# Sliding-window attention on one core: score matmuls in eight tiles of 32 rows by 64 keys, and another order of the first quarter's Q and K

## The chip, the cores and the metric

The kernel runs on one core of one Trainium2 chip. The metric is the device time of that core in microseconds, from the launch to the last output byte. Engines are named as the profile names them: PE is the matmul engine and PEld its weight loads, DVE the vector engine, ACT the scalar engine, POOL the GpSimd engine, SP the engine that issues most transfers.

## The reference

Two independent problems A and B have the same shape: `x` is 2048 tokens by 1024 channels, `wqkv` 1024 by 3072, `wo` 1024 by 1024, all in bf16. Each is causal attention with 32 heads of 32 channels in a window of 256 keys; the two outputs stand side by side.

```python
H = 32; Dh = D // H; W = 256
qkv = ((x @ wqkv).reshape(B, S, 3, H, Dh)).transpose(2, 0, 3, 1, 4)
q, k, v = qkv[0], qkv[1], qkv[2]
scores = einsum("bhqd,bhkd->bhqk", q, k) * (Dh ** -0.5)
mask = (idx[:, None] - idx[None, :] >= 0) & (idx[:, None] - idx[None, :] < W)
scores = where(mask, scores, -1e9)
o = einsum("bhqk,bhkd->bhqd", softmax(scores), v)
return o.transpose(0, 2, 1, 3).reshape(B, S, D) @ wo
```

## The kernel before

The work is cut into 16 groups `g` (2 problems times 8), each of four heads: four heads of 32 channels fill 128 partitions. Tokens are cut into 16 blocks of 128. Keys stand on the partitions of a score tile and queries in its columns. A block `j` of keys meets the query blocks `q = j`, `j + 1` and `j + 2` alone; such a pair (g, j, q) is an entry. A group has 45 entries. Four entries at a time make a session, 180 in all.

`session(now)` computes one. It takes the score tile `st` (128 partitions, 4 heads, 4 entries, 128 queries in f32, four banks of PSUM, pool `ps_st` with one buffer). Entries of one key block that follow each other form a segment, with one matmul a head: 32 rows of `kT` and `qT` against 128 keys, at the row tile of that head (L451):

```python
for r in range(4):
    nc.tensor.matmul(
        st[:, r, a:b, :],
        lhsT=kT[32 * r:32 * r + 32, j * P:(j + 1) * P],
        rhs=qT[32 * r:32 * r + 32, q * P:(q + b - a) * P],
        start=True, stop=True, tile_position=(32 * r, 0))
```

A segment has one to three entries, so 128, 256 or 384 columns. In most sessions the segments are three and one, two and two, or one and three entries; twelve sessions at the seams of groups have three segments. ACT then takes the exponential of the whole tile into `pt` in bf16 (L459), and POOL clears what lies outside the mask in the entries with `q = j` (L467) and `q = j + 2` (L471). DVE adds the two edge blocks of a query block for the sums (L481).

`pv` multiplies the probabilities of a pair of query blocks by V and by ones (L513, column tiles of 32: each of the four heads writes its own 32 partitions). DVE normalises (L524, L529, L531). All projections (Q, K, V, output) accumulate in `pp`, a pool `ps_proj` of two banks. Their matmuls go through `by_columns`: whole 128x128 matmuls (L172), or, where a `pv` follows the session, four column tiles of 32 (L176). `evacuate` copies a finished `pp` to SBUF on ACT (L190) or DVE (L192), whichever a small clock in the program holds to be free earlier; `add_or` keeps a running OR of Q and K for a range test (L184).

The order of the instructions on each engine is written out by the program. For each session the loop emits the scores, then what `pv` and edge sums are due, then as many projection matmuls as `level` gives it from due times of chains (a chain is one accumulation over 8 channel tiles). Weights and x come by transfers that SP issues, planned by sessions too.

The head of the kernel has an order of its own. The first 512 tokens of A's x come as four row blocks `xrow[a]` and are transposed on PE (`flip`, L583), and ACT (L587) and DVE (L588) copy the halves of a transposed block to `xT`, one after the other. The other quarters come by transposing transfers (L133). `keep_warm` fills PE's waits with matmuls on zeros (L569), written to a part of the first `st` tile. The transfers stand in this order: Q's weights of group 0 on ACT's queue; on SP's queue x block 0, K's weights, x blocks 1 to 3, V's weights, the next quarter of x. Q and K of the first quarter (`first(a)`) are computed 128 tokens at a time behind each transposed block, Q then K, each accumulating in its own `pp` bank:

```python
flip(0); keep_warm(3); first(0)
flip(1); keep_warm(2); flip(2); first(1)
flip(3); first(2); first(3)
emit(0, chains[0].size)
```

The last line emits the first V chain. The sessions follow.

## Time and profile before

| what | value |
|---|---|
| median of 4 runs | 610.06 us (609.48 to 610.48) |
| the profiled execution | 610.16 us, span 608.4 us |
| PE busy, instructions | 598.9 us (98%), 12868 matmuls |
| PEld / DVE / ACT / POOL busy | 57% / 77% / 72% / 54% |
| score matmuls (L451) | 1488 |
| exponential (L459) | 180, 1878 ns each |
| first scores start | 14.27 us |

The span is what the profiler records from the first to the last instruction of the program; the profiled execution's time holds about 1.7 us more. A busy PE includes the tails of matmuls that overlap, so its share says who is busy and not how well; for the length of a stage, the starts of the matmuls are read. A group of instructions in the profile is given by its line, engine, operation, output and inputs.

### The profile page before, as it was taken

The numbers are of one execution on the slowest core, as the hardware profiler recorded it, in microseconds if no ns is written. First come the engines' busy times: TensorE is split into PE (matmuls) and PEld (weight loads), VectorE is DVE, ScalarE is ACT, GpSimd is POOL, SyncE is SP. The second block draws the span as 40 slices with busy tenths as digits, with TensorE's granted clock in tenths as the row PEclk, the third lists the DMA queues.
The fourth block names the chain that finished last, engine by engine and source line by source line (L and its number), as shares of the span: only waits on it lengthen the run. The fifth ranks groups of instructions, "written<-read, shape, count | busy, mean of one in ns | idle before, by whom it ended". The sixth has DMA issues, their size and how long they took to land.

```text
span 608.4 us, 28879 instructions
## 1 busy us (share of the span) xinstructions
PE 598.9 (98%) x12868; PEld 344.5 (57%) x12868; DVE 469.0 (77%) x1200; ACT 440.6 (72%) x375; POOL 326.2 (54%) x630
## 2 busy tenths in 40 slices
PE   8999999999999999999999999999999999999996
PEld 5555466656655756564556756655455665545443
DVE  2577889998898898897888887898888887887200
ACT  3777888788888887877778877777776777785332
POOL 0565666665666666556555565555555655554000
PEclk9999999999999999999999999999999999999998
DMA  9833110111015601553111100112021030113221
GB/s 236 181 88 91 37 39 3 38 37 39 3 38 90 118 9 28 86 96 80 37 37 38 38 4 10 31 37 81 2 64 37 6 104 20 56 62 115 72 78 64
DMA packets 86802, 35.47 MB, mean 58 GB/s; under 512 B 65552, under 2 KB 86160, under 8 KB 86672
## 3 DMA queue, kind: packets, MB, share of 16 engines
q1 hardware_dynamic: 85632, 33.31, 22.6%
q8 instruction: 102, 1.67, 1.1%
q10 hardware_dynamic: 1040, 0.26, 0.2%
q14 instruction: 28, 0.23, 0.1%
HBM read 17.83 MB, written 8.39 MB: 43 GB/s over the span
## 4 chain that ended last, share of the span: by engine, by line
PE 96%; ACT 2%; DMA 1%; SPq 0%; issue 0%; ACTq 0%
PE pp L176 43%; PE pp L172 29%; PE acc L513 13%; PE st L451 10%; ACT pt L459 1%; DMA oT<-in_A_x_dram 1%; PE acc L583 0%; ACT vt L190 0%; ACT kT L190 0%; ACT qT L190 0%; PE st L583 0%; PE st L569 0%; SPq L145 0%; SPq L548 0%; ACT osb L190 0%
## 5 line engine op out<-in xcount | busy, mean ns | idle before, releaser
L459 ACT ACTIVATE pt<-st 128x2048 bf16<-128x2048 f32 x180 | 338.0, 1878 | 91.9 <-PE st L451 72.7
L471 POOL TENSOR_SCALAR_AFFINE_SELECT pt<-pt 128x512 bf16<-128x512 bf16 x224 | 154.4, 689 | 145.5 <-ACT pt L459 144.0
L467 POOL TENSOR_SCALAR_AFFINE_SELECT pt<-pt 128x512 bf16<-128x512 bf16 x256 | 179.0, 701 | 86.5 <-ACT pt L459 85.6
L524 DVE RECIPROCAL rinv<-acc 128x128 f32<-128x128 f32 x128 | 121.9, 953 | 57.0 <-PE acc L513 56.5
L176 PE MATMUL pp<-xT,wqk 128*32 128x512 bf16 x2712 | 163.1, 379 | 0.0
L481 DVE TENSOR_TENSOR both<-pt 128x512 bf16<-128x512 bf16 x224 | 137.1, 651 | 0.0
L176 PEld LDWEIGHTS <-wqk 128*32 128x32 bf16 x2712 | 69.3, 97 | 54.2 <-issue 0.4
L172 PE MATMUL pp<-xT,wqk 128*128 128x512 bf16 (+1 forms) x394 | 83.4, 354 | 0.9 <-ACT vt L190 0.5
L176 PE MATMUL pp<-wv,xT 128*32 128x256 bf16 x2436 | 75.9, 273 | 0.0
L451 PE MATMUL st<-qT,kT 32*128 32x384 bf16 (+2 forms) x1488 | 71.5, 269 | 0.0
L176 PEld LDWEIGHTS <-xT 128*32 128x32 bf16 x2436 | 63.8, 97 | 6.1
L529 DVE STREAM_SHUFFLE wide<-rinv 128x128 f32<-128x128 f32 x256 | 64.6, 298 | 0.0
L513 PE MATMUL acc<-pt,vt 128*32 128x128 bf16 (+1 forms) x2160 | 63.3, 239 | 0.0
L172 PE MATMUL pp<-wo_sb,oT 128*128 128x512 bf16 (+1 forms) x282 | 61.2, 373 | 0.0
L451 PEld LDWEIGHTS <-kT 32*128 32x128 bf16 x1488 | 22.2, 92 | 64.5 <-issue 63.2
L190 ACT CAST osb<-pp 128x512 bf16<-128x512 f32 (+1 forms) x52 | 30.0, 576 | 39.1 <-PE pp L172 25.5
L531 DVE TENSOR_TENSOR oT<-acc,wide 128x256 bf16<-128x256 f32 x128 | 54.3, 424 | 4.4
L176 PE MATMUL pp<-wo_sb,oT 128*32 128x512 bf16 x952 | 55.6, 379 | 0.0
L172 PEld LDWEIGHTS <-wqk 128*128 128x128 bf16 x394 | 34.2, 98 | 37.5 <-issue 6.8
L172 PE MATMUL pp<-wv,xT 128*128 128x256 bf16 x415 | 50.9, 273 | 1.3 <-ACT kT L190 0.6
L513 PEld LDWEIGHTS <-vt 128*32 128x32 bf16 x2160 | 35.9, 96 | 26.4 <-issue 24.1
L172 PEld LDWEIGHTS <-xT 128*128 128x128 bf16 x415 | 39.0, 98 | 12.3 <-issue 6.4
(46 smaller groups left out, 385.0 us busy)
## 6 DMA issues: line engine op xcount, KB each, us to landing
out_dram<-osb SPq DMA_DIRECT2D x63, 128.0 KB, 1.8
wqk<-in_B_wqkv_dram SPq DMA_DIRECT2D x32, 128.0 KB, 2.6
wqk<-in_A_wqkv_dram SPq DMA_DIRECT2D x24, 128.0 KB, 2.8
wo_sb<-in_A_wo_dram SPq DMA_DIRECT2D x16, 128.0 KB, 2.2
wv<-in_B_wqkv_dram SPq DMA_DIRECT2D x16, 128.0 KB, 2.5
wo_sb<-in_B_wo_dram SPq DMA_DIRECT2D x16, 128.0 KB, 2.2
oT<-in_A_x_dram SPq DMA_DIRECT2D x4, 256.0 KB, 5.5
wv<-in_A_wqkv_dram SPq DMA_DIRECT2D x2, 512.0 KB, 5.9
```

The source lines that it names most:

```text
L172: nc.tensor.matmul(out[:, lo:hi], lhsT=lhsT, rhs=rhs, start=start, stop=stop, skip_group_check=True)
L176: nc.tensor.matmul(out[c:c + 32, lo:hi], lhsT=lhsT[:, c:c + 32], rhs=rhs, start=start, stop=stop, tile_position=(0, c), skip_group_check=True)
L190: nc.scalar.copy(out=out, in_=in_)
L451: nc.tensor.matmul(st[:, r, a:b, :], lhsT=kT[32 * r:32 * r + 32, j * P:(j + 1) * P], rhs=qT[32 * r:32 * r + 32, q * P:(q + b - a) * P], st ...
L459: nc.scalar.activation(out=pt[:, :, :n, :].rearrange("p r a q -> p r (a q)"), in_=st[:, :, :n, :].rearrange("p r a q -> p r (a q)"), func= ...
L467: nc.gpsimd.affine_select(out=blk, in_=blk, pattern=[[0, 4], [1, P]], compare_op=ALU.is_ge, fill=0.0, base=0, channel_multiplier=-1)
L471: nc.gpsimd.affine_select(out=blk, in_=blk, pattern=[[0, 4], [-1, P]], compare_op=ALU.is_gt, fill=0.0, base=0, channel_multiplier=1)
L481: nc.vector.tensor_tensor(out=both[:, :, h, :], in0=pts[s0][:, :, a0, :], in1=pts[s1][:, :, a1, :], op=ALU.add)
L513: nc.tensor.matmul(acc[32 * r:32 * r + 32, o:o + w_], lhsT=lhsT, rhs=src[:, r, :, :], start=(x == 0), stop=(x == len(moves) - 1), tile_pos ...
L524: nc.vector.reciprocal(out=rinv[:], in_=acc[:, 2 * P:3 * P])
L529: nc.vector.stream_shuffle(out=wide[:, h * P:(h + 1) * P], in_=rinv[:], mask=[16 * h] * 32)
L531: nc.vector.tensor_tensor(out=oTs[(pi, k)][:, t, (p % 2) * 256:(p % 2 + 1) * 256], in0=acc[:, 0:256], in1=wide[:], op=ALU.mult)
```

## The change

The score matmul of a segment and head becomes two, one for each half of its 128 keys. A half has a tile of 32 rows by 64 columns of the array and writes 64 partitions, so a segment has eight tiles. Each half goes over just the queries that it can meet: the upper 64 keys leave out the first 64 queries of an entry with `q = j`, the lower 64 keys the last 64 queries of an entry with `q = j + 2`. The score tile is one tile for the whole kernel, `scores`, cleared once by two memsets on DVE; the parts left out hold earlier scores, which the exponential covers and POOL clears with the mask.

In the head, `keep_warm` writes to a `pp` tile. K's weights are transferred behind x block 1 in place of ahead of it. Q and K of the first quarter are computed 256 tokens at a time: the first two transposes, Q's first half, the other two transposes, K's first half, then Q's and K's second halves. Lines behind line 19 of the new kernel are moved by a few; its scores are L458, its exponential L466, its P·V L520.

```diff
+HALF = 64
...
-        st = ps_st.tile([P, 4, SLOTS, P], F32, name="st")
+        st = scores
+        flat = st[:].rearrange("p r a q -> p r (a q)")
...
-            for r in range(4):
-                nc.tensor.matmul(
-                    st[:, r, a:b, :],
-                    lhsT=kT[32 * r:32 * r + 32, j * P:(j + 1) * P],
-                    rhs=qT[32 * r:32 * r + 32, q * P:(q + b - a) * P],
-                    start=True, stop=True, tile_position=(32 * r, 0))
+            for c in range(2):
+                lo = HALF if c == 1 and q == j else 0
+                hi = (b - a) * P - (HALF if c == 0 and q + b - a == j + 3 else 0)
+                keys = slice(j * P + c * HALF, j * P + (c + 1) * HALF)
+                for r in range(4):
+                    rows = slice(32 * r, 32 * r + 32)
+                    nc.tensor.matmul(
+                        flat[c * HALF:(c + 1) * HALF, r, a * P + lo:a * P + hi],
+                        lhsT=kT[rows, keys], rhs=qT[rows, q * P + lo:q * P + hi],
+                        start=True, stop=True, tile_position=(32 * r, c * HALF),
+                        skip_group_check=True)
...
-        if a == 0:
+        if a == 1:
             load_wqk(0, 1, nc.sync)
...
-    spare = ps_st.tile([P, 4, SLOTS, P], F32, name="st")[:].rearrange("p r a q -> p r (a q)")
-    warm = spare[:, 1]
+    scores = ps_st.tile([P, 4, SLOTS, P], F32, name="st")
+    nc.vector.memset(scores[:, 1:4], 0.0)
+    warm = ps_proj.tile([P, 512], F32, name="pp")
...
-    flips.append(spare[:, 0])
+    flips.append(scores[:, 0].rearrange("p a q -> p (a q)"))
...
-    def first(a):
-        for which in range(2):
-            for _, f in qk_steps(0, which, 0, a * P, (a + 1) * P, held[which], last=a == QB - 1):
-                f()
+    def first(which, lo):
+        for _, f in qk_steps(0, which, 0, lo, lo + 256, held[which], last=lo > 0):
+            f()
 
     flip(0)
+    keep_warm(4)
+    flip(1)
     keep_warm(3)
-    first(0)
-    flip(1)
-    keep_warm(2)
+    first(0, 0)
     flip(2)
-    first(1)
     flip(3)
-    first(2)
-    first(3)
+    nc.vector.memset(scores[:, 0:1], 0.0)
+    first(1, 0)
+    first(0, 256)
+    first(1, 256)
     emit(0, chains[0].size)
```

## The prediction

> **What bounds the kernel now.** I read the page first: its engine table, the chain that ended last, then the waits.

> ```profile
> span 608.4 us, 28879 instructions
> ...
> PE 598.9 (98%) x12868; PEld 344.5 (57%) x12868; DVE 469.0 (77%) x1200; ACT 440.6 (72%) x375; POOL 326.2 (54%) x630
> ...
> PEclk9999999999999999999999999999999999999998
> ...
> PE 96%; ACT 2%; DMA 1%; SPq 0%; issue 0%; ACTq 0%
> PE pp L176 43%; PE pp L172 29%; PE acc L513 13%; PE st L451 10%; ACT pt L459 1%; DMA oT<-in_A_x_dram 1%; PE acc L583 0%; ACT vt L190 0%; ACT kT L190 0%; ACT qT L190 0%; PE st L583 0%; PE st L569 0%; SPq L145 0%; SPq L548 0%; ACT osb L190 0%
> ```

> TensorE (PE) carries 96% of the chain that ended last, at the full clock; DVE, ACT and POOL have slack of 23% and more. The waits say the same from the other side:

> ```profile
> ACT pt L459 <- PE st L451: 72.7, 112, 1.3
> PEld L451 <- issue: 63.2, 177, 0.4
> PE pp L172 <- ACT vt L190: 1.0, 2, 0.5
> ```

> The columns are total us, times, longest us. The exponential (L459) waits for the scores (L451); no line has PE waiting for L459. So what a score session takes on PE adds straight to the span, 180 times. One session in the timeline of PE (start, us, instructions):

> ```profile
> 299.74 0.60 PE L172 MATMUL pp<-wv,xT 128*128 128x256 bf16 x4
> 300.27 0.40 PE L451 MATMUL st<-qT,kT 32*128 32x128 bf16 x8
> 300.60 0.51 PE L513 MATMUL acc<-pt,vt 128*32 128x128 bf16 x16
> 300.94 0.28 PE L513 MATMUL acc<-pt,ones 128*32 128x128 bf16 x8
> 301.05 0.28 PE L513 MATMUL acc<-both,ones 128*32 128x128 bf16 x8
> 301.17 1.16 PE L176 MATMUL pp<-wv,xT 128*32 128x256 bf16 x36
> ```

> Starts are the reading; a duration holds the pipeline's tail. Eight L513 matmuls of 128 moving columns take 0.11 us: two groups of four column tiles, 56 ns a group. Groups of 256 start 109 ns apart, of 512 columns 216: so a group costs 0.417 ns a column and 2.5 ns. Within a group the four starts are 3.3 ns apart. The session starts a change of tile shape on both sides. From the end of the stream ahead (299.74 plus four times 109 ns = 300.18) to the first L513 at 300.60 it takes 0.42 us; by the starts behind the rows, 423 ns in the 168 sessions of two segments (421 to 433), whatever the split. Its terms: 96 ns until the first score starts; the second segment starts 66, 119 or 173 ns after the first (128, 256, 384 columns), about 10.4 over the stream's 56, 109, 162, which is the one weight load that nothing hides; then the stream, and about 100 ns until the next shape starts. So 213 of the 423 ns are moving columns.

> **The score blocks.** Score matmuls double from 1488 to 2976, in eight tiles (four row groups by two halves of 64 keys). Each column half streams its own queries. Per session the longer half has 448 columns in 172 sessions (448 and 384 where three or one entries stand first, 448 and 448 for two and two) and 512 in eight of the twelve with three segments: mean 450.8 for 512. If the halves run side by side, that is 61.2 columns, 25.5 ns, times 180: −4.6 us. Against it: (a) The first weight load now has 64 columns and no group ahead to hide it. [...] I take twice 10.4: +10.4 ns times 180 = +1.9 us. [...] (b) The second half starts four pairs behind, 4 x 3.3 = 13.2 ns, which shows where it is as long as the first or longer: 56 sessions of two and two and 52 of one and three, 108 x 13.2 = +1.4 us. At half the spacing it is +0.7, at double +2.8 and some more of it in the others. Sum −1.3 us. With both costs at the kind end the same count, tile by tile, gives −4.8; with a load of 26.7 ns and double spacing +3.2.

> The change of shape on both sides stays: as many switches, in the same order.

> [...]

> **One score tile for good.** It replaces a new tile a session; with one buffer before, each session waited for the exponential ahead then as now. That wait costs nothing today: no session exceeds 433 ns. Unwritten parts hold old finite scores; the exponential covers the same 128x2048 and POOL's selects are the same 480. Two memsets are added on DVE. By the 0.27 us of the 128x256 memset they take 1.6 and 0.55 us. The first lies in DVE's idle time before 5.46 us, the second after the last transposed copy, over 2 us before the first scores that wait for it. Cost nothing; uncovered, 0.5.

> **The head.** The rest of the order on PE, DVE, ACT, POOL and SP is the same.

> ```profile
> 5.48 0.84 PE L172 MATMUL pp<-xT,wqk 128*128 128x128 bf16 x8
> 6.53 0.62 PE L172 MATMUL pp<-xT,wqk 128*128 128x128 bf16 x8 [0.21 <-DMA wqk<-in_A_wqkv_dram]
> 7.21 0.62 PE L583 MATMUL acc<-ident,oT 128*128 128x128 bf16 x8
> 7.87 0.58 ACT L587 COPY xT<-acc 128x512 bf16<-128x512 bf16 x1 [2.44 <-PE acc L583]
> 8.48 0.42 DVE L588 COPY xT<-acc 128x512 bf16<-128x512 bf16 x1 [2.60 <-ACT xT L587]
> 10.07 2.12 PE L172 MATMUL pp<-xT,wqk 128*128 128x128 bf16 x32
> 11.79 0.58 ACT L190 CAST qT<-pp 128x512 bf16<-128x512 f32 x1 [0.93 <-PE pp L172]
> 12.43 1.91 PE L172 MATMUL pp<-wv,xT 128*128 128x256 bf16 x16 [0.23 <-ACT qT L190]
> ```

> The second x block lands at 7.16 behind K's weights (6.48); Q's weights land at 5.36, and later x blocks 0.68 to 0.71 us apart (7.84, 8.55). Moved ahead, it should land near 5.36 + 0.68 = 6.04 (earliest about 5.2, latest K's old slot 6.48), and K's weights at 7.16, wanted only after 9 us. Landing to the end of ACT's copy is 1.29 us in the rows, so 7.33; Q's first half (8 x 109 ns, its second part behind DVE's copy) ends at 8.28; the two remaining transposes of 0.45 us reach 9.17; K's first half ends at 10.04. ACT's two copies end at 9.51 and 10.10, DVE's at 10.55; Q's second half runs 10.12 to 11.04, K's to 11.91. Q's cast then ends at 11.82, so the V chain starts at 11.91 for 12.43: −0.5 us. The ends, 5.2 and 6.48, give −0.8 and −0.2. K's cast moves from DVE to ACT, where it ends before 12.8, ahead of the scores at 13.7. What is late next: the next x quarter lands at 15.38 and would be wanted at 15.7 instead of 16.2, so it just does not bind.

> **Sum.** −1.3 − 0.5 = −1.8 us on the profiled execution's 610.16 us (span 608.4), which is 0.10 above the median 610.06: 608.3.

> **Rivals.** *Given back*: load at 26.7 ns (blocks −0.2 us), head −0.2 to −0.8: 609.0 to 609.6. For it: three small terms cancel. *Every load exposed* (slower): the 64-column loads do not hide behind the other half's matmuls, so each of the four groups of a session shows 20.8 ns: 83 − 10.4 − 25.5 = +47 ns, times 180 = +8.5, with the head +8.0: 618.1. It decides from 10 ns a session on, half of one load. For it: no row of the trace holds 64-column loads, nor row and column tiles together; against it, loads of the next segment start 11 to 21 ns into the first. *Serial halves* (slower): 853.3 columns in place of 512, +142 ns, +25.6 us, with load and head +27.0: 637.1. Against it: row tiles run side by side in L451, column tiles in L513.

> **How the numbers follow.** A measurement of this kernel tells about 0.2% (1.2 us) from no change. Forecast 0.48, its own range 604.5 (−4.8 and −0.8) to 608.8; given back 0.15; every load exposed 0.24; serial 0.13. The range takes in the third case and leaves the serial one and the ends: 604.5 to 618.5. Faster 0.48, same 0.15, slower 0.37.

> **What would show it.** Right: session blocks of about 416 ns, the second half's scores starting 13 ns after the first's, the first V chain near 11.9 us. Wrong: a second half that starts a stream later (serial), second segments later than their stream by a load (exposed), a V chain still at 12.4, or a new wait of PE on L466.

## The result, and the profile after

The changed kernel takes 610.93 us (median of 32 runs, 609.76 to 611.84), the kernel before 610.04 us (52 runs, 609.48 to 610.93). The ratio is 1.0013, 95% interval 1.0008 to 1.0018: slower by about 0.8 us, where 1.8 us less was forecast. Its runs also spread over 2.1 us, those of before over 1.45. The profiled execution took 610.33 us (span 608.6), one of the faster ones. First its page:

```profile
span 608.6 us, 31799 instructions
...
PE 599.0 (98%) x14326; PEld 352.2 (58%) x14326; DVE 470.8 (77%) x1201; ACT 441.1 (72%) x376; POOL 325.9 (54%) x630
...
q8 instruction: 114, 1.87, 1.2%
...
PE 97%; ACT 2%; issue 0%; DVE 0%; ACTq 0%
...
L458 PE MATMUL st<-qT,kT 32*64 32x320 bf16 (+4 forms) x2976 | 71.2, 259 | 0.5 <-issue 0.5
...
L458 PEld LDWEIGHTS <-kT 32*64 32x64 bf16 x2976 | 29.1, 103 | 65.3 <-issue 64.4
```

PE still carries the chain. Queue q8 moves instructions: 114 packets and 1.87 MB, 16 KB each. Of the page of before, the lines that answer to it:

```profile
q8 instruction: 102, 1.67, 1.1%
...
L451 PEld LDWEIGHTS <-kT 32*128 32x128 bf16 x1488 | 22.2, 92 | 64.5 <-issue 63.2
```

Twelve packets more. Who made PE wait, in the changed kernel (columns as before: total us, times, longest us):

```profile
PE pp L577 <- DVE top L126: 1.3, 1, 1.3
PE pp L173 <- ACT vt L191: 1.1, 2, 0.5
PE pp L173 <- ACT kT L191: 0.6, 2, 0.4
PE st L458 <- issue: 0.5, 1, 0.5
PE acc L520 <- issue: 0.4, 1, 0.4
```

The last two lines are new. "issue" is time in which PE waited for nothing that the profile shows. A session without such a wait, in the timeline of PE:

```profile
299.93 0.82 PE L173 MATMUL pp<-wv,xT 128*128 128x256 bf16 x6
300.68 0.40 PE L458 MATMUL st<-qT,kT 32*64 32x64 bf16 x16
301.01 0.51 PE L520 MATMUL acc<-pt,vt 128*32 128x128 bf16 x16
301.35 0.28 PE L520 MATMUL acc<-pt,ones 128*32 128x128 bf16 x8
301.46 0.29 PE L520 MATMUL acc<-both,ones 128*32 128x128 bf16 x8
```

Sixteen matmuls take from 300.68 to 301.01, 0.33 us, as eight did: this is a session of one and three entries. Read from the starts behind the rows, from the end of the stream ahead to the next shape: sessions of three and one fell from 423 to 407 ns, those of two and two and of one and three by 2 to 3 ns, eight of the twelve with three segments rose by 11. Now two places with the new wait:

```profile
27.94 0.50 PE L520 MATMUL acc<-pt,vt 128*32 128x128 bf16 x13
28.81 0.23 PE L520 MATMUL acc<-pt,vt 128*32 128x128 bf16 x3 [0.37 <-issue]
28.82 0.34 PE L520 MATMUL acc<-pt,ones 128*32 128x128 bf16 x8
...
209.97 0.35 PE L458 MATMUL st<-qT,kT 32*64 32x64 bf16 x10
210.83 0.34 PE L458 MATMUL st<-qT,kT 32*64 32x320 bf16 x6 [0.51 <-issue]
```

PE stops in the middle of a group of tiles, after 13 of 16 and after 10 of 16 matmuls, for 0.6 and 0.8 us from start to start, and the instruction that comes next waits for no semaphore. Counted among PE's records, the first instruction behind a stop is number 705 here, 10433 there, and 3777 at a smaller one at 87.98 us. (Weight loads and waits for semaphores are counted as well.) Each is 193 more than a multiple of 256, so they lie whole multiples of 256 apart, and the packets come to some 250 instructions each: 102 for 25,736 matmuls and loads before, 114 for 28,652 now. So the stops stand at the seams of the pieces in which PE's instructions arrive.

Counted at those seams, in both traces, there is one transfer for every piece: PE begins a piece, a transfer on q8 starts 0.50 us later (median in the changed kernel; nine in ten lie between 1.6 us before and 1.6 after), takes 0.99 us, and, by this count, brings the piece that follows. The soonest use after a landing is 1.35 us, and five of the six shortest, 1.35 to 1.45 us, are the pieces for which PE waited. One behind the other the three make some 2.9 us, an estimate. The densest pieces of the changed kernel last 2.97 us, of the kernel before 3.07; there the soonest use is 1.6 us after landing, and no wait of PE on "issue" stands in that profile. The stop at 28.8 us differs from the others: its piece follows one that lasted 6.4 us, so the stream was not dense there, but the transfer started only 3.99 us after PE had begun that piece (3.12 in the kernel before): at 26.41 us, against 26.43 before, though PE came to that piece 0.9 us sooner. What held it is not shown.

The sum of the two profiles, from start to start of PE's work: first scores −0.85 us, blocks −1.11, stops +0.92 inside blocks and +0.92 outside, other stretches between blocks +0.39; together +0.27 us at the last matmul. The 0.39 lies in eleven stretches that lose 16 to 50 ns each. In every one the loss stands at a single matmul that a cast releases (ten on ACT, L191, and one on DVE), mostly by freeing a `pp` bank, and the cast comes no earlier although the block is shorter.

### The profile page after: what moved, and what is told of

It reads as the page before. It is cut to its first block, busy times and chain, and to the rows that moved or that the text cites. A ratio compares the mean times of both kernels' runs of the same rounds, so it can differ in the third digit from the quotient of the medians.

```text
span 608.6 us, 31799 instructions
## 1 busy us (share of the span) xinstructions
PE 599.0 (98%) x14326; PEld 352.2 (58%) x14326; DVE 470.8 (77%) x1201; ACT 441.1 (72%) x376; POOL 325.9 (54%) x630
## 2 busy tenths in 40 slices
DMA packets 86814, 35.67 MB, mean 59 GB/s; under 512 B 65552, under 2 KB 86160, under 8 KB 86672
## 3 DMA queue, kind: packets, MB, share of 16 engines
q8 instruction: 114, 1.87, 1.2%
## 4 chain that ended last, share of the span: by engine, by line
PE 97%; ACT 2%; issue 0%; DVE 0%; ACTq 0%
PE pp L177 44%; PE pp L173 29%; PE acc L520 14%; PE st L458 10%; ACT pt L466 1%; PE pp L577 1%; PE acc L591 0%; ACT kT L191 0%; ACT vt L191 0%; PE st L591 0%; ACT osb L191 0%; DVE top L126 0%; PE pp L815 0%; DVE ones L791 0%; ACTq L191 0%
## 5 line engine op out<-in xcount | busy, mean ns | idle before, releaser
L466 ACT ACTIVATE pt<-st 128x2048 bf16<-128x2048 f32 x180 | 338.0, 1878 | 94.6 <-PE st L458 75.0
L173 PE MATMUL pp<-xT,wqk 128*128 128x512 bf16 (+1 forms) x362 | 82.5, 370 | 0.6 <-ACT vt L191 0.5
L458 PE MATMUL st<-qT,kT 32*64 32x320 bf16 (+4 forms) x2976 | 71.2, 259 | 0.5 <-issue 0.5
L458 PEld LDWEIGHTS <-kT 32*64 32x64 bf16 x2976 | 29.1, 103 | 65.3 <-issue 64.4
L520 PE MATMUL acc<-pt,vt 128*32 128x128 bf16 (+1 forms) x2160 | 63.6, 239 | 0.4 <-issue 0.4
L173 PE MATMUL pp<-wo_sb,oT 128*128 128x512 bf16 (+1 forms) x282 | 61.2, 373 | 0.0
L191 ACT CAST osb<-pp 128x512 bf16<-128x512 f32 (+1 forms) x52 | 30.0, 576 | 38.6 <-PE pp L173 25.5
L520 PEld LDWEIGHTS <-vt 128*32 128x32 bf16 x2160 | 35.9, 96 | 21.5 <-issue 19.1
```

What stands on the lines that cost most here:

```text
L173: nc.tensor.matmul(out[:, lo:hi], lhsT=lhsT, rhs=rhs, start=start, stop=stop, skip_group_check=True)
L191: nc.scalar.copy(out=out, in_=in_)
L458: nc.tensor.matmul(flat[c * HALF:(c + 1) * HALF, r, a * P + lo:a * P + hi], lhsT=kT[rows, keys], rhs=qT[rows, q * P + lo:q * P + hi], star ...
L466: nc.scalar.activation(out=pt[:, :, :n, :].rearrange("p r a q -> p r (a q)"), in_=st[:, :, :n, :].rearrange("p r a q -> p r (a q)"), func= ...
L520: nc.tensor.matmul(acc[32 * r:32 * r + 32, o:o + w_], lhsT=lhsT, rhs=src[:, r, :, :], start=(x == 0), stop=(x == len(moves) - 1), tile_pos ...
```

## The experiments

Theory: instruction supply, as above. Rival: the earlier head, which runs PE into transfers of x. Ratios are to the kernel before, run beside each kernel, with 95% intervals. "Stops" are the differences of over 60 ns to the profile of before, inside a session's block or between two blocks, added up.

**Scores alone (e1).** The changed `session` with the head of before:

```diff
+    scores = ps_st.tile([P, 4, SLOTS, P], F32, name="st")
+    nc.vector.memset(scores[:, 2:4], 0.0)
+    spare = scores[:].rearrange("p r a q -> p r (a q)")
...
+    nc.vector.memset(scores[:, 0:2], 0.0)
     first(2)
     first(3)
```

> The eight-tile scores alone, with the head of before (the one score tile is cleared in two parts, half of it behind the last transposed copy). Theory, instruction supply: PE's instructions come in transfers of 256, and the denser stream reaches the end of a piece before the next is there. The blocks give 1.1 us as in the changed kernel's profile, and stalls of PE without a semaphore, each at the end of a piece of 256, take 1.5 to 2.5 us: 610.4 to 611.4 us. Rival, the earlier head: the stalls come from the head that runs 0.85 us early into the transfers of x; without it the blocks' gain shows whole, 608.9 us, and no stalls of that kind.

Ratio 1.0024 (1.0015 to 1.0033), median 611.73 for 610.42 us. The edit had a cost of its own: PE's first matmuls, which write the same tile, waited for the first clearing and began at 2.48 us instead of 1.31; first scores came 0.84 us late. So this run does not tell the theories apart by its time. Its profile (613.58 us, its slowest execution) has blocks −1.12 us and stops of 3.2 us. Of these, 0.72 us at 262.88 stand at no seam and end just after transfers of x and of V's weights land; the others, 2.5 us, stand at seams.

**Scores alone, cleared late (e5).** The two memsets become one behind the last transposed copy.

> The eight-tile scores alone again, with the whole score tile cleared behind the last transposed copy, so that nothing of the first microseconds differs from the kernel before (in the first form half of the clearing stood ahead of PE's first matmuls and moved them 1.2 us). Instruction supply: head 0, blocks -1.1 us, stalls 1.5 to 3 us: 0.4 to 1.9 us over the kernel before. Rival, that the loss of the first form was its late start alone: 1.1 us under the kernel before.

Ratio 1.0014 (1.0005 to 1.0023). The profiled execution, the fastest of its eleven at 609.93 us, shows blocks −1.07 us and stops of 0.67 us. The scores alone, with the order of the head as before, are slower although the blocks are shorter in sum. The earlier head as the whole cause is out.

**Head alone (e2).** The changed kernel with the four-tile loop of L451 put back.

> The new order of the head alone, with the four-tile scores of before. Instruction supply: fewer instructions by then, so PE reaches the end of the third piece (near 28.8 us in the changed kernel) later, and stalls little; the head's 0.85 us stay: 609.2 us (609.0 to 609.6). Rival, the earlier head: the stall near 28 us is there again and takes 0.6 us or more: 609.8 us and above.

Ratio 0.9988 (0.9979 to 0.9998), median −0.63 us; no stretch between its blocks is longer by more than 60 ns, no stop near 28 us. So the head alone does not make that stop. But it has a part in it: the stop near 28.8 us stands in the profiles of the changed kernel, e7, e8, e9 and e10 (0.59, 0.21, 0.36, 0.10 and 0.44 us), which have the new head and eight tiles in most sessions, and in none with only one of the two. The head gains, a little less than expected. Why, its profile shows; the four filling matmuls, first in it:

```profile
5.15 1.68 PE L571 MATMUL pp<-top 128*128 128x512 bf16 x4
6.67 0.61 PE L585 MATMUL acc<-ident,oT 128*128 128x128 bf16 x8
```

and then in the changed kernel:

```profile
4.81 1.05 PE L577 MATMUL pp<-top 128*128 128x512 bf16 x4
5.85 0.62 PE L591 MATMUL acc<-ident,oT 128*128 128x128 bf16 x8
```

The same four take 1.68 us in one execution, 1.05 in the other: the trace's record of the full granted clock begins at 6.47 us in e2, at 4.85 us in the changed kernel, at 4.09 us in the kernel before, and the starts of these matmuls lie 0.43 us apart ahead of it and 0.22 behind it. x block 1 had landed at 6.15 us in e2, but the filling was not done until 6.67.

**Twice the instructions, same tiles (e3).** The kernel before, each score matmul cut by columns:

```diff
-            for r in range(4):
+            w2 = (b - a) * P // 2
+            for c in range(2):
+                for r in range(4):
...
+                        flat[:, r, a * P + c * w2:a * P + (c + 1) * w2],
...
+                        rhs=qT[32 * r:32 * r + 32, q * P + c * w2:q * P + (c + 1) * w2],
```

> The kernel before with each score matmul cut into two by its columns: the same four row tiles, columns and order, but 2976 score matmuls and weight loads as in the changed kernel. Instruction supply: 2.5 ns a group more (0.9 us in all) and stalls as in the changed kernel, 1.5 to 3 us: 612.4 to 614.0 us, with stalls at the ends of pieces of 256. Rival, the tile shape or the head: 0.9 us alone, 610.9 us, no stalls.

Ratio 1.0037 (1.0023 to 1.0051), 2.2 us. The block rose by 5 ns as counted (0.91 us in the profile); stops of 1.39 us stand beside it. Of these, 0.36 us at 262.68 stand at no seam and end just after transfers of x and of V's weights land; the other 1.03 us stand at seams, half a microsecond of it here:

```profile
283.64 0.22 PE L516 MATMUL acc<-both,ones 128*32 128x128 bf16 x1
284.14 0.29 PE L516 MATMUL acc<-both,ones 128*32 128x128 bf16 x7 [0.28 <-issue]
```

Old tiles, old head, and the stops are there: they come with the number of instructions.

**Four times the instructions (e6).** The same with four parts.

> The kernel before with each score matmul cut into four by its columns: 5952 score matmuls, nothing else changed. Groups cost 3 x 2.5 ns more for each of two segments, 15 ns a session, 2.7 us. Instruction supply: the stalls grow faster than the count, from 1.5 us with two parts to 3 to 8 us: 6 to 11 us over the kernel before. Rival, that short matmuls cost a fixed time each: 2.7 us over it, no stalls.

Ratio 1.0449 (1.0413 to 1.0485): 26.6 us, over twice the upper end. Its page and its PE timeline at one session:

```profile
span 635.7 us, 37754 instructions
...
q8 instruction: 137, 2.24, 1.5%
```

```profile
396.84 0.29 PE L454 MATMUL st<-qT,kT 32*128 32x64 bf16 x15
397.42 0.40 PE L454 MATMUL st<-qT,kT 32*128 32x64 bf16 x33 [0.28 <-issue]
```

Differences over 60 ns in its blocks and between them add up to 21 us. The rest is the block itself, which rose by 44 ns in the median and not 15: in the sessions of two and two, whose parts have 64 columns, it rose by the 15 expected, so parts of 32 columns cost more than their columns. However dense the stream, transfers on q8 start no closer than 3.3 us here, 3.3 in the changed kernel and 3.1 before.

**Without the later weight transfers (e7).** Every instruction of PE, ACT and DVE as in the changed kernel; the weights of V go the same way as those of Q and K below, and POOL's small clears ahead of the transfers with them:

```diff
-        fs = [lambda g=g: new_wqk(g)]
+        fs = [lambda g=g: wqk.__setitem__(g, wqk[g - 2])]
```

> The changed kernel without the transfers of the Q, K and V weights from the third group on (it reuses the weights of the first groups, so most of the output is that of other weights); every instruction of PE, ACT and DVE is as in the changed kernel. Instruction supply, late because other transfers stand ahead of the fetch: the stalls that follow a late start of the fetch (near 78, 87, 210 us) go, those below 40 us can stay; 0.7 to 1.6 us under the kernel before. If the fetch is too slow by itself for so dense a stream, whatever else is moved: stalls as in the changed kernel, 0.5 us and more over the kernel before.

Ratio 1.0013 (1.0004 to 1.0022), the changed kernel's own, with 25.17 MB moved for 35.67. The session at 210 us stops as in the changed kernel, though for less:

```profile
210.00 0.69 PE L457 MATMUL st<-qT,kT 32*64 32x64 bf16 x16
210.62 0.83 PE L173 MATMUL pp<-wv,xT 128*128 128x256 bf16 x6
```

0.62 us where a session takes 0.33. I had given both outcomes; it is the second: the supply is too slow without these transfers too, though those of x, the output weights and the output remain. Its profile has stops of 1.2 us for 1.8; whether the traffic lengthens single ones, two executions do not settle, and in the time no gain can be seen.

**Longer half first (e8).**

```diff
-            for c in range(2):
+            for c in ((1, 0) if q > j and q + b - a == j + 3 else (0, 1)):
```

> The changed kernel with the longer half issued first where a segment ends with the far edge (q = j + 2) and does not begin on the diagonal. If the lag of 13 ns of the second half is what took the gain of the sessions with one and then three entries, they fall from -2 to about -16 ns, 52 x 13 ns = 0.7 us less than the changed kernel, with the same number of instructions and the same kind of stalls: from 0.6 us under to 0.6 us over the kernel before. If the tiles do not run apart, nothing changes in the blocks.

Ratio 1.0017 (1.0007 to 1.0027). The blocks did as expected: sessions of one and three fell to 407 to 410 ns as well, all blocks −1.75 us. The time did not. A cheaper block makes the pieces denser still; its profile has 1.5 us of stops, at 609.67 us the fastest of nine executions.

**Eight tiles where they pay (e4, e9).** e4 keeps them in the 56 sessions of three and one; e9 in the 112 of three and one or one and three, with the longer half first. The others have the loop of before:

```diff
+            eight = es[0][:2] == es[2][:2] or es[1][:2] == es[3][:2]
+            for c in (() if not eight else (1, 0) if q > j and q + b - a == j + 3 else (0, 1)):
```

> The changed kernel with eight tiles only in the sessions with three entries and then one (56 of 180, where the block gained 16 ns against 2 ns in the others), and the four tiles of before in the rest. Blocks -0.9 us, head -0.85 us, a third of the added instructions. Instruction supply: stalls under 0.8 us in all: 608.4 to 609.1 us. Rival, the earlier head: stalls as in the changed kernel near 28 and 80 to 90 us: 609.4 us and above.

> The kernel with the longer half first, with eight tiles in the 112 sessions of three and one or one and three entries alone; the sessions of two and two (where eight tiles gained 2 ns) and those of three segments have four tiles again. Head -0.65 us, blocks 112 x 15 ns = -1.7 us, +0.4 us where PE then waits for a cast on ACT, 62% of the added instructions. Instruction supply: stalls of 0.3 to 1.2 us are left: 0.7 to 1.6 us under the kernel before. Rival, that the stalls do not follow the instructions: as with eight tiles everywhere, 0.5 us and more over it.

Ratios 0.9987 (0.9978 to 0.9996) and 0.9986 (0.9977 to 0.9995): faster than both kernels, but not to be told from the head alone. In e9's profile the blocks give 1.73 us; stops and longer stretches outside them take 1.77 us back. e4's shows no stop over 60 ns and −0.87 us in blocks, of which its median shows 0.13 us beyond the head's.

**The dense chains elsewhere (e10, e11).** V chains in column tiles put eight instructions into 109 ns. e10 takes them first where they run as whole matmuls, on top of e8; e11 does the same with four-tile scores.

```diff
+        fit = [n for n in ready if chains[n].dense == whole[0]]
+        n = fit[0] if fit and chains[ready[0]].late > now + 2 else ready[0]
```

> The kernel with the longer half first and eight tiles everywhere, and another choice of the next chain: V chains (column tiles of 256 columns, eight instructions in 109 ns) are taken first in sessions without P.V, where they run as whole 128x128 matmuls, and others first in sessions with P.V, as long as nothing is due within two sessions. Column-tiled V matmuls fall from 2436 to 1188. Instruction supply: the densest stretches of PE's stream go, and the stalls with them (under 0.5 us): head -0.65, blocks -1.75, waits for ACT +0.4, together 1.5 to 2.0 us under the kernel before. Rival: nothing changes in the stalls, 0.3 to 1.0 us over it.

> The same choice of chains with the head alone and the four-tile scores of before: what the other order does by itself. Instruction supply: there were no stalls to take away, so as the head alone, 0.3 to 1.0 us under the kernel before. If the order gains by itself (fewer waits for casts), 1.5 us and more under it, and the kernel with eight tiles owes its time to that.

e10: 0.9994 (0.9985 to 1.0003); e11: 0.9989 (0.9980 to 0.9998). The order does nothing for four tiles (0.9988 for the head alone), and takes eight tiles from 1.0017 to 0.9994, intervals that do not meet. It also takes 486 matmuls out of both kernels, so density and number fall together. So the time followed the density of the stream in the expected direction, but not all stops went: e10's profile still has two, of 0.44 us at 29.1 and 0.64 us at 207.5 us. It stayed short of its expected 1.5 to 2.0 us.

The best versions, e2, e4, e9 and e11, lie within 0.03% of each other: all have the new head, none gets more from the scores.

## Why the prediction was wrong

*The scores side by side: right, a little too good.* Blocks −1.11 us for −1.3. The halves run apart, the second starts 13 ns behind the first as counted, and e8 shows that this lag cost what it was priced at. For the first load of 64 columns the sum has 20.8 ns, twice the 10.4 of the profile of before: an estimate of mine that no run shows. It came to 24 ns: first segments of 64, 192 and 320 columns end 53, 106 and 160 ns after their start for streams of 29, 82.5 and 136. The 26.7 ns of "given back" is 64 columns at the 0.417 ns a column of the streams; no run shows it for a load either. The rivals of serial halves and of every load exposed did not happen; where a session has three segments, the third follows the second by its stream alone (133 and 189 ns into the block for 128 columns), so one load shows in a session and not four. The ends given for this sum, −4.8 and +3.2, do not come out of its terms: −4.6 + 0 + 0.7 (nothing more for the load, half the spacing) is −3.9, and −4.6 + 2.9 + 2.8 is 1.1 and some more. The first sets the low end of the range; neither bears on what failed.

*The head: right.* The V chain began at 11.58 us for 11.91 forecast and 12.43 before:

```profile
5.85 0.62 PE L591 MATMUL acc<-ident,oT 128*128 128x128 bf16 x8
7.15 1.05 PE L173 MATMUL pp<-xT,wqk 128*128 128x256 bf16 x8
...
8.93 2.81 PE L173 MATMUL pp<-xT,wqk 128*128 128x256 bf16 x24
10.90 0.58 ACT L191 CAST qT<-pp 128x512 bf16<-128x512 f32 x1 [1.14 <-PE pp L173]
...
11.58 1.91 PE L173 MATMUL pp<-wv,xT 128*128 128x256 bf16 x16
```

V no longer waits for Q's cast. Over the runs of e2 the head is worth 0.63 us for 0.5. That the two are so close is in part luck: the forecast had no term for the moment at which the granted clock rises, and in the executions of e2 and e4, where that came at 6.47 and 6.97 us, the first scores began at 14.23 and 14.47 us, against 14.27 before.

*The step that failed* is in the score blocks' sum: of the 2916 instructions more in PE's stream (12868 to 14326 matmuls, each with a load), only the spacing inside a block, 3.3 ns a pair, was priced. Bringing them in was set at nothing without naming what hides it, and no case had it. The runs put stops at the seams of the instruction pieces in its place: 1.8 us in the changed kernel's profile, 0.7 to 2.5 us in the other profiles with all the added instructions and the program's order as it was (e5 and e1 the ends), and by the medians 0.89 + 0.63 + 1.11 − 0.39 = 2.2 us, if nothing else differs. The first of them, at 28.8 us, also took back 0.6 of the 0.85 us of the head in that execution: PE came to the seam earlier, the piece did not. "Given back" came nearest, 1.3 us short at its upper end, and for another reason.

The profile of before held the warning: q8's 102 packets of 16 KB are PE's 25,736 matmuls and loads in pieces of 256, and its densest piece of 3.07 us was used 1.6 us after landing, 0.2 to 0.4 us over the soonest uses in the traces with the added instructions (1.2 to 1.4 us).

*Open.* That a stop is a late piece rests on where it stands, on the landings, and on e3, e6 and e10; the supply itself was not changed, as no run had larger pieces or an earlier request. What the 1.35 us between landing and use consist of, and why some transfers start late, as that ahead of 28.8 us does, no trace shows. The 0.6 us by which the median run lies over the profiled one was not seen in a profile.

## What to carry to other kernels

On a saturated PE count instructions as well as columns: in these thirteen traces no piece of 256, loads included, passed in under 2.9 us, so a tiling that doubles a matmul's instructions to save an eighth of its columns should sit where the stream around it is thin. Look at the instruction queue in the profile, find the seams of its pieces, and see how little room the densest piece leaves. A wait on "issue" in the middle of a group of tiles, at the same count modulo 256 (193 in the changed kernel), was the sign here; the two stops at other counts, 0.72 us in e1 and 0.36 us in e3, ended just after a landing.
